# A fused SSD and cos-gated feed-forward kernel: hp in seven products in three steps of chunks 2, 3 and 4 as well

## Chip, cores, metric

One core of a Trainium2 chip. The metric is the device time of one execution in microseconds, lower is better. A time is the median of several executions; one further execution was profiled.

## The reference, cut to what matters

```python
# x (4, 8, 768, 32), a (4, 8, 768), B and C (4, 8, 768, 16); w_in (256, 2048), w_out (2048, 256); all fp32
# first block, per sequence and head, in chunks of the time axis:
log_a = np.log(np.clip(a, 1e-06, 1.0));  cum = np.cumsum(la, axis=-1)
L = np.exp(cum[:, :, :, None] - cum[:, :, None, :]) * causal
y_intra = einsum('bhij,bhjd->bhid', einsum('bhin,bhjn->bhij', Cc, Bc) * L, xc)
y_inter = einsum('bhin,bhnd->bhid', Cc, state) * np.exp(cum)[..., None]
y[:, :, sl] = y_intra + y_inter          # and state is carried to the next chunk
# second block, on y as (3072, 256):
h = y @ w_in
g = h * np.cos(h)
out = g @ w_out
```

The change touches the product y @ w_in, and the small differences that it needs.

## The kernel before

**Tiling.** The time axis of 768 is cut into six chunks of 128 (c = 0 to 5). A chunk holds 512 rows of the second block. The feed-forward runs in steps n = 0 to 95; step n belongs to chunk c = n // 16, with f = n % 16. In chunks 1 to 5 a step takes one half of the chunk's rows, u = f // 8 (256 rows), and one eighth of d_ff, j = f % 8 (256 columns of w_in). A tile hp of a step is 128 partitions by 512 columns, one PSUM bank.

**One step.** `first(n)` makes hp with four fp32 matmuls of 256 columns (L660). `wind_k` (ACT, L667) and `wind_w` (DVE, L673) reduce the argument of the cosine, `gate` (ACT, L682) takes the Sin, `gated` (DVE, L687) multiplies hp and cosine into gT. `second(n - 2)` then multiplies the gT of two steps earlier with w_out.

**Seven products.** A product of two 2x2 block matrices can be had with seven block products in place of eight, if differences and sums of the blocks are ready (Strassen's way, in Winograd's form). For o, `seven(n)` does so in every step from chunk 1 on: seven matmuls of 128 columns (L835). Its differences of gT are made in `differ(n)` on POOL (L712, L714, L715), those of w_out in `differ_w`. After the eight steps of a half chunk ACT copies the seven accumulators to ps (`take`, L847 and L848), four additions make the result (`rest`, L860: on DVE in most places, on POOL in others) and SP stores it (L863).

For hp, `first7(n)` (L759) does the same in steps 81 to 93 only, the range `sevens`. It needs differences of w_in (`differ_in`, POOL, L731, 16 instructions spread over chunks 3 and 4) and of y (`differ_y`, DVE, L741, step 79). The parts are put together by an ACT copy of the first product (L766) and four DVE additions (L772, L775, L777, L780). A step in `sevens` gates the step before it: `first_of_seven(n)` runs `wind_k(n - 1)` and the rest between and after the seven products, since hp is whole only after the additions. The step after the last of the range gates two.

**PSUM.** hp alternates between two banks (tag "h"). Within a run of seven products every third hp takes a third one, the first half of a pair of banks of the tag "scan"; the other pair of that tag holds four 128x128 accumulators of `first7` (the tile m of `pair("m")`). The two pairs of "scan" are also those of the first block's products: `inner2` (L603, f = 5), `open2` (L617, L477, f = 13) and `finish2` (L629, f = 15) compute the next chunk's y while the present chunk is in the feed-forward. o has two banks.

**Work of the first block on DVE.** Of the next chunks: `reaches` (f = 1, 2), `turn_blocks` (3, 4), `weights` (6, 7; L465), and the scans of `decays2` (8, 9, 10, 11; L375), each pair of which is followed by a load of new decay rows on SP (L165) and a product on POOL (`weigh0`, L381). `unsummed` holds the `rest` of a half chunk until its turn; in regular steps all four additions are run at once on DVE, but not in steps 10 and 11; in steps of `sevens` one addition a step on POOL.

**Order.** The program order on each engine is written out by hand in the loop over n; an engine takes its instructions in that order, and semaphores come from the data and the buffers. On SP the loads of coming chunks and the stores stand in one queue.

Of the kernel before, what the change touches and what calls it, by code (L numbers as in the profile page):

```python
# [12 lines left out]
ALU = mybir.AluOpType  # L13
# [12 lines left out]
def kernel(  # L26
# [13 lines left out]
    V, ACT, G, PE = nc.vector, nc.scalar, nc.gpsimd, nc.tensor  # L40
# [3 lines left out]
    P = 128  # L44
    NC = S // P
    DM, DF = moe_w_in.shape
    KT = DM // P
    NF = DF // P
# [28 lines left out]
    along, blocks = {}, {}  # L77
# [205 lines left out]
    for s in range(2):  # L283
# [3 lines left out]
        out=a_in, in_=a.rearrange("(u b) h (c p) -> (b h c) u p", u=NU, p=P))  # L287
# [67 lines left out]
    reach, part, yT, after = {}, {}, {}, {}  # L355
# [287 lines left out]
    NJ = NF // 2  # L643
# [78 lines left out]
    def differ_in(i, js):  # L722

        if i == len(wid):
            t = conv.tile([P, 2 * WC, 2], U32, tag="words", bufs=8, name="wid")
            wid.append(t.rearrange("p a w -> p (a w)").bitcast(FP32)
                       .rearrange("p (j f) -> p j f", j=NJ))
        g = [win4[:, k, js, e] for k in range(2) for e in range(2)]
        a_ = (g[1], g[1], g[0], g[2])[i]
        b_ = (g[3], g[0], wid[0][:, js], wid[min(i, 2)][:, js])[i]  # L730
        G.tensor_tensor(out=wid[i][:, js], in0=a_, in1=b_, op=ALU.subtract)  # L731

    def differ_y(c, i):

        if i == 0:
            yd[c] = ms[2].rearrange("p (i u m) -> p i u m", i=4, u=2)
        d = yd[c]
        y11, y12, y21, y22 = (yT[c][:, :, k, h * P:(h + 1) * P] for k in range(2) for h in range(2))
        a_ = (y12, y22, y22, y21)[i]
        b_ = (y11, y12, d[:, 0], d[:, 2])[i]  # L740
        V.tensor_tensor(out=d[:, i], in0=a_, in1=b_,  # L741
                        op=ALU.add if i in (1, 2) else ALU.subtract)

    def first7(n, to_, at6, at, between):

# [219 lines left out]
    def rest_of_loads():  # L965
# [21 lines left out]
        for k in (4, 5):  # L987
            for s in range(2):
# [4 lines left out]
    steps = {c: dict(reach=(5, 6), turn=(6, 7), inner=8, weigh=(9, 10), state=(-NF, 12),  # L993
                     decays=(8, 11, 13, 14), along=(12, 13)) if c == 2 else
             dict(reach=(1, 2), turn=(3, 4), inner=5, weigh=(6, 7), state=(0, 5),
                  decays=(8, 9, 10, 11), along=(6, 7)) for c in range(2, NC)}
    first_decays = (NF + 1, NF + 2, NF + 3, NF + 4)

    def chunks_at(n, what):
# [20 lines left out]

    sevens = range(NC * NF - 15, NC * NF - 2)
    late, at_ = [], {}
    quiet = (5, 6, 7, 8, 9, 10, 13, 14)

    def first_of_seven(n):

        i = n - sevens[0]
        if i == 0:  # L1030
            at_["hp"] = pair("hp")[:, 0]
            at_["m"] = pair("m").rearrange("p b (q m) -> p b q m", m=P)
        if n == NC * NF - NJ + LAG + 1:
            at_["hp"] = bank([P, TB], "hp", "o")
        to_ = at_["hp"] if i % 3 == 1 else bank([P, TB], "hp", "h")
        if n not in sevens:
            first(n, to_=to_)
            return
        sums, last_sum = first7(n, to_, at_["m"][:, 1, 0], at_["m"][:, 0],
                                lambda: wind_k(n - 1) if i else None)  # L1040
        if i:
            wind_w(late[0])
        sums()
        gate(late[0]) if i else None
        gated(late.pop())
        last_sum()
# [55 lines left out]
    for n in range(AHEAD, NC * NF + LAG):  # L1102
        c, f = divmod(n, NF)
        if n < NC * NF:

            if c > 0 and f in (loads_of := (6, 7, 8, 9) if c == 1 else (0, 1, 2, 3)):
                load(c + 2, loads_of.index(f))
            if n in (NF - 4, NF - 3):
                load_arow(n - NF + 8)
            if n == NF - 2:  # L1110
                for k in (4, 5):
                    for s in range(2):
                        load_x(k, s)
            if n in (NF - 1, NF):
                load_along(2, (2 * (n == NF), 2 * (n == NF) + 1))
            for e, i in chunks_at(n, "along"):
                load_along(e + 1, (2 * i, 2 * i + 1))
            if n in sevens or n - 1 in sevens:
                first_of_seven(n)
            else:  # L1120
                first(n)
            if n not in sevens and n - 1 in sevens:
                wind(n - 1)
                gate(n - 1)
                gated(late.pop())
            closing = f == NF - 1 and 1 <= c < NC - 1
            take_y = finish2(c + 1) if closing else None
            if n not in sevens:
                wind_k(n)
                wind_w(n)  # L1130
            if closing:
                take_y(0)
            for e, s in chunks_at(n - 1, "turn"):
                turn2(e, s)
            for k in units_at(n, 2):
                turn_unit(k)
            if n + 1 in piece:
                rests_of.append(grade(*piece[n + 1], later=True))
            if n not in sevens:
                gate(n)  # L1140
            while len(rests_of) > (n == AHEAD):
                rest = rests_of.pop(0)
                if rest:
                    rest()
            joins = n in piece and piece[n] in held
            if joins:
                join(*piece[n])

            behind = [lambda at=at: decays2(*at) for at in decays_at(n)]
            behind += [lambda k=2 * c - 1 + i: add_state(k) for c, i in chunks_at(n, "state")]  # L1150
            behind += [lambda c=c, b=2 * s + p: reaches(c, b) for c, s in chunks_at(n, "reach")
                       for p in range(2)]
            behind += [lambda at=at: turn_blocks(*at) for at in chunks_at(n, "turn")]
            behind += [lambda k=k, p=p: decays0(k, p) for k, at in unit_at.items()
                       for p in range(2) if at[0][p] == n]
            behind = [lambda k=2 * c + i, q=q: weights(k, q) for c, i in chunks_at(n, "weigh")
                      for q in range(2)] + behind
            behind = [lambda k=k: weights(k, 1) for k in units_at(n - 1, 3)] + behind
            if not joins and behind:
                behind.pop(0)()  # L1160
            if n + 1 in sevens or n in sevens:
                late.append(n)
            else:
                gated(n)
            if closing:
                take_y(1)
            if n == NF + 7:
                weigh0(5)
            if add_s and (n == NF - 5 or units_at(n - 1, 4)):
                exchange = add_s()  # L1170
                add_s = None
            if n == NF + 9:
                exchange()
            for do in behind:
                do()
            for i in range(4 if n == sevens[0] - 2 else 0):
                differ_y(NC - 1, i)
            if n in sevens and unsummed:
                unsummed[0](range(summed[0], summed[0] + 1), G)
                summed[0] = (summed[0] + 1) % 4  # L1180
                if summed[0] == 0:
                    unsummed.pop()
            if n not in sevens and f not in ((10, 11, 12) if c == 1 else (10, 11)):
                for do in unsummed:
                    do()
                unsummed.clear()
            for k, ((_, last_), *_) in unit_at.items():
                if last_ == n:
                    weigh0(k)
        for i, js in differ_at.get(n, ()):  # L1190
            differ_w(i, js)
        if NC - 3 <= c < NC - 1 and f in quiet:
            i, q = divmod((c - NC + 3) * len(quiet) + quiet.index(f), 4)
            differ_in(i, slice(2 * q, 2 * q + 2))
        if n == AHEAD + 1:
            second(AHEAD - LAG)
        if n >= LAG and n != AHEAD:
            second(n - LAG)
        for e, _ in chunks_at(n, "inner"):
            inner2(e)  # L1200
        for k in units_at(n, 3):
            for t in range(2):
                inner(k, t)
            if k == 3:
                at = [gs[k, s][:, 0, 2 * P:] for s in range(2)]
                sums(4, at, group)
                take_sums((4,), at)
            weights(k, 0)
        for k in units_at(n, 4):
            take_s, add_s = finish0(k)  # L1210
            take_s()
        for k in units_at(n, 1):
            reach_unit(k)
        if f == NF - 3 and 1 <= c < NC - 1:
            open2(c + 1)
        for at, e in block_loads.items():
            if at == n:
                loading = load_blocks(e)
            if at <= n < at + 12:
                next(loading)  # L1220
# [30 lines left out]
```

## Time and profile before

| | |
|---|---|
| median of 3 runs | 365.75 us (365.31 to 366.82) |
| the profiled execution, its own time | 365.62 us |
| its span | 363.8 us, 10001 instructions |
| PE (TensorE matmul) busy | 358.3 us, 98% |
| weight loads (PEld, beside PE) | 325.7 us, 90% |
| DVE busy | 262.2 us, 72% |
| POOL busy | 220.8 us, 61% |
| ACT busy | 180.9 us, 50% |
| L660 hp, four products | 664 records, 158.2 us |
| L835 o, seven products | 1106 records, 14 a step |
| L759 hp, seven products | 182 records in 13 steps |

How to read it: an fp32 matmul leaves two records, so four matmuls of `first` are eight records. Records overlap, since matmuls are pipelined, and the mean of one is longer than its share of the time; the chain of waits in order of time gives the share. The difference of 1.8 us between the execution's time and its span lies outside of the instructions. A row of the profile's groups names line, engine, operation, output <- inputs, shape and count, then busy time, mean of one, and idle time before it with what ended it. "Idle before" of an engine that nobody waits for costs nothing.

### The profile page before, as it was taken

The numbers are of one execution on the slowest core, as the hardware profiler recorded it, in microseconds if no ns is written. First come the engines' busy times: TensorE is split into PE (matmuls) and PEld (weight loads), VectorE is DVE, ScalarE is ACT, GpSimd is POOL, SyncE is SP. The second block draws the span as 40 slices with busy tenths as digits, with TensorE's granted clock in tenths as the row PEclk, the third lists the DMA queues.
The fourth block names the chain that finished last, engine by engine and source line by source line (L and its number), as shares of the span: only waits on it lengthen the run. The fifth ranks groups of instructions, "written<-read, shape, count | busy, mean of one in ns | idle before, by whom it ended". The sixth has DMA issues, their size and how long they took to land.

```text
span 363.8 us, 10001 instructions
## 1 busy us (share of the span) xinstructions
PE 358.3 (98%) x3980; PEld 325.7 (90%) x3980; DVE 262.2 (72%) x468; ACT 180.9 (50%) x337; POOL 220.8 (61%) x355
## 2 busy tenths in 40 slices
PE   8999999999999999999999999999999999999995
PEld 5788888888999999999989999999999999999995
DVE  7789988488777856977735878654877456688874
ACT  3587757444455255535335544425453534544642
POOL 5567747579767543447733458945456746475562
PEclk9999999999999999999999999999999999999999
DMA  8995957692665445315124121010010010001001
GB/s 142 254 372 132 183 128 131 105 135 61 120 100 78 92 99 84 57 46 113 21 50 70 35 56 27 0 41 10 2 31 0 2 29 4 2 1 31 1 14 46
DMA packets 97326, 26.41 MB, mean 73 GB/s; under 512 B 87328, under 2 KB 93184, under 8 KB 97280
## 3 DMA queue, kind: packets, MB, share of 16 engines
q1 hardware_dynamic: 96032, 25.38, 34.6%
q8 instruction: 31, 0.51, 0.6%
q10 hardware_dynamic: 1248, 0.39, 0.5%
q14 instruction: 15, 0.12, 0.1%
HBM read 22.36 MB, written 3.34 MB: 71 GB/s over the span
## 4 chain that ended last, share of the span: by engine, by line
PE 89%; DVE 4%; POOL 3%; ACT 2%; issue 2%; ACTq 0%; POOLq 0%; DVEq 0%
PE hp L660 36%; PE o L835 33%; PE o L795 5%; PE m L759 3%; PE hp L759 2%; PE y L629 2%; PE g L603 1%; DVE mag L261 1%; PE y L477 1%; PE y L617 1%; DVE mag L263 1%; POOL gd L714 1%; PE a_ps L364 1%; POOL gd L712 1%; PE g L456 1%
## 5 line engine op out<-in xcount | busy, mean ns | idle before, releaser
L660 PE MATMUL hp<-yT,w_in 128*128 128x256 f32 x664 | 158.2, 382 | 0.4 <-DVE gT L687 0.4
L660 PEld LDWEIGHTS hp<-yT,w_in 128*128 128x128 f32 x664 | 120.6, 190 | 16.5 <-issue 1.3
L712 POOL TENSOR_TENSOR gd<-gT 128x256 f32<-128x256 f32 x79 | 59.9, 758 | 94.7 <-DVE gT L687 84.5
L673 DVE SCALAR_TENSOR_TENSOR w<-hp,k 128x512 f32<-128x512 f32 x96 | 65.9, 687 | 58.1 <-ACT k L667 58.0
L682 ACT ACTIVATE w<-w,quarter 128x512 f32<-128x512 f32 x96 | 69.4, 723 | 69.5 <-DVE w L673 69.2
L667 ACT ACTIVATE k<-hp 128x512 int32<-128x512 f32 x96 | 57.1, 595 | 83.0 <-PE hp L660 79.8
L687 DVE TENSOR_TENSOR gT<-hp,w 128x512 f32<-128x512 f32 x96 | 65.6, 683 | 24.0 <-ACT w L682 22.1
L835 PE MATMUL o<-words,gd 128*128 128x128 f32 x474 | 66.1, 275 | 0.1
L835 PEld LDWEIGHTS o<-words,gd 128*128 128x128 f32 x474 | 59.3, 192 | 0.4 <-POOL gd L714 0.3
L835 PEld LDWEIGHTS o<-w_out,gT 128*128 128x128 f32 x316 | 46.8, 191 | 3.5
L835 PE MATMUL o<-w_out,gT 128*128 128x128 f32 x316 | 49.7, 276 | 0.0
L715 POOL TENSOR_TENSOR gd<-gT,gd 128x128 f32<-128x128 f32 x79 | 41.2, 522 | 6.2
L714 POOL TENSOR_TENSOR gd<-gT,gd 128x128 f32<-128x128 f32 x79 | 40.6, 514 | 6.2
L835 PE MATMUL o<-w_out,gd 128*128 128x128 f32 x158 | 30.6, 276 | 0.0
L835 PE MATMUL o<-words,gT 128*128 128x128 f32 x158 | 30.5, 275 | 0.0
L795 PE MATMUL o<-w_out,gT 128*128 128x256 f32 x128 | 29.9, 379 | 0.0
L375 DVE TENSOR_TENSOR_SCAN lam<-arow,unit 128x512 f32<-128x512 f32 x20 | 28.0, 1402 | 0.0
L795 PEld LDWEIGHTS o<-w_out,gT 128*128 128x128 f32 x128 | 24.2, 190 | 3.3
L835 PEld LDWEIGHTS o<-words,gT 128*128 128x128 f32 x158 | 24.0, 192 | 0.0
L835 PEld LDWEIGHTS o<-w_out,gd 128*128 128x128 f32 x158 | 24.0, 192 | 0.0
L465 DVE TENSOR_TENSOR m<-g,lam 128x512 f32<-128x512 f32 x24 | 16.2, 681 | 0.7 <-PE g L456 0.5
L271 POOL TENSOR_TENSOR w_out<-mag,last 128x512 uint32<-128x512 uint32 x8 | 10.2, 1276 | 10.1 <-DVE mag L263 10.1
(128 smaller groups left out, 373.3 us busy)
## 6 DMA issues: line engine op xcount, KB each, us to landing
words<-in_moe_w_in_dram SPq DMA_DIRECT2D x8, 512.0 KB
words<-in_moe_w_out_dram SPq DMA_DIRECT2D x8, 512.0 KB
xr<-in_x_dram SPq DMA_DIRECT2D x24, 128.0 KB
arow<-a_cut SPq DMA_DIRECT2D x10, 256.0 KB
arow<-a_cut SPq DMA_DIRECT2D x10, 252.0 KB
out_dram<-sum SPq DMA_DIRECT2D x18, 128.0 KB
bc<-in_B_dram SPq DMA_DIRECT2D x24, 64.0 KB
blocks<-in_B_dram SPq DMA_DIRECT2D x16, 32.0 KB
```

What stands on the lines that cost most here:

```text
L375: V.tensor_tensor_scan(out=lams[k][:, p, hs].rearrange(flat), data0=rows_.rearrange(flat), data1=unit0[:, hs].rearrange(flat), initial=0.0 ...
L660: PE.matmul(to_[:, e], lhsT=w_in[:, k, fs], rhs=y[:, k], start=(k == 0), stop=(k == KT - 1), skip_group_check=True)
L667: ACT.activation(k, hp[n], AF.Copy, bias=0.25, scale=INV_2PI)
L673: V.scalar_tensor_tensor(out=w, in0=hp[n], scalar=INV_2PI, in1=k, op0=ALU.mult, op1=ALU.subtract)
L682: ACT.activation(cos, cos, AF.Sin, bias=quarter, scale=TWO_PI)
L687: V.tensor_tensor(out=gT[n], in0=hp.pop(n), in1=cos, op=ALU.mult)
L712: G.tensor_tensor(out=d[:, 0:2], in0=g[:, 1:2].to_broadcast([P, 2, P]), in1=g[:, 3::-3], op=ALU.subtract)
L714: G.tensor_tensor(out=d[:, 2], in0=g[:, 0], in1=d[:, 0], op=ALU.subtract)
L715: G.tensor_tensor(out=d[:, 3], in0=g[:, 2], in1=d[:, 2], op=ALU.subtract)
L759: PE.matmul(dst[q], lhsT=w[q], rhs=y_[q], start=(q in (6, 1, 7)), stop=True, skip_group_check=True)
L795: PE.matmul(o[c, u][:, t], lhsT=g[:, 2 * e + t], rhs=w_out[:, 2 * j + e], start=(j == e == t == 0), stop=(j == NJ - 1 and e == 1), skip_gr ...
L835: PE.matmul(at[q], lhsT=a_[q], rhs=w[q], start=(j == 0 and q in starts), stop=(j == NJ - 1), skip_group_check=True)
```

## The change

Nine more steps make hp in seven products: f = 10 to 12 (u = 1, j = 2 to 4) of chunks 2, 3 and 4, that is steps 42 to 44, 58 to 60 and 74 to 76. What goes with it:

- The differences of w_in are made earlier and in three parts by columns: j = 2 to 4 in steps 27 to 30 (four instructions of 128x384), j = 0 and 1 in steps 45 to 48 (four of 128x256), j = 5 to 7 in steps 61 to 64 (four of 128x384). The 16 instructions of 128x256 in chunks 3 and 4 go.
- The differences of y for chunks 2, 3 and 4, of half u = 1 only, are made on POOL in steps f = 4 to 7, one each (128x128). For chunk 5 they stay on DVE in step 79.
- Two of the four scans `decays` of chunks 4 and 5 move from f = 10, 11 to f = 14, 15, with the load of decay rows and the `weigh0` that follow them. `along` and the rest stay.
- The sums of the half chunk that ends at f = 7 are made on POOL in steps f = 10 to 13, one addition a step, in place of all four on DVE in step f = 12; the copies to ps are issued within `first7` of step f = 10 and not at the end of step f = 9.

```diff
-    def differ_y(c, i):
+    def differ_y(c, i, eng, us=slice(0, 2)):
...
-        V.tensor_tensor(out=d[:, i], in0=a_, in1=b_,
-                        op=ALU.add if i in (1, 2) else ALU.subtract)
+        eng.tensor_tensor(out=d[:, i, us], in0=a_, in1=b_,
+                          op=ALU.add if i in (1, 2) else ALU.subtract)
...
-                  decays=(8, 9, 10, 11), along=(6, 7)) for c in range(2, NC)}
+                  decays=(8, 9, 14, 15), along=(6, 7)) for c in range(2, NC)}
...
-    sevens = range(NC * NF - 15, NC * NF - 2)
+    runs = [*(range(NF * c + 10, NF * c + 13) for c in range(2, NC - 1)),
+            range(NC * NF - 15, NC * NF - 2)]
+    sevens = {n: r for r in runs for n in r}
     late, at_ = [], {}
-    quiet = (5, 6, 7, 8, 9, 10, 13, 14)
 
     def first_of_seven(n):
 
-        i = n - sevens[0]
+        i = n - sevens.get(n, sevens.get(n - 1))[0]
...
-            for i in range(4 if n == sevens[0] - 2 else 0):
-                differ_y(NC - 1, i)
-            if n in sevens and unsummed:
+            if n == runs[-1][0] - 2:
+                for i in range(4):
+                    differ_y(NC - 1, i, V)
+            if 2 <= c < NC - 1 and 4 <= f <= 7:
+                differ_y(c, f - 4, G, slice(1, 2))
+            if unsummed and (n in sevens or summed[0]):
                 unsummed[0](range(summed[0], summed[0] + 1), G)
                 summed[0] = (summed[0] + 1) % 4
                 if summed[0] == 0:
                     unsummed.pop()
-            if n not in sevens and f not in ((10, 11, 12) if c == 1 else (10, 11)):
+            elif n not in sevens and f not in ((10, 11, 12) if c == 1 else (10, 11)):
...
-        if NC - 3 <= c < NC - 1 and f in quiet:
-            i, q = divmod((c - NC + 3) * len(quiet) + quiet.index(f), 4)
-            differ_in(i, slice(2 * q, 2 * q + 2))
+        for start, js in zip((2 * NF - 5, 3 * NF - 3, 4 * NF - 3),
+                             (slice(2, 5), slice(0, 2), slice(5, NJ))):
+            if start <= n < start + 4:
+                differ_in(n - start, js)
```

More of the change, by code (lines that the diff above doesn't have):

```diff
@@ L737, in differ_y @@
         d = yd[c]
-        y11, y12, y21, y22 = (yT[c][:, :, k, h * P:(h + 1) * P] for k in range(2) for h in range(2))
+        y11, y12, y21, y22 = (yT[c][:, us, k, h * P:(h + 1) * P] for k in range(2)
+                              for h in range(2))
         a_ = (y12, y22, y22, y21)[i]
-        b_ = (y11, y12, d[:, 0], d[:, 2])[i]
-        V.tensor_tensor(out=d[:, i], in0=a_, in1=b_,
-                        op=ALU.add if i in (1, 2) else ALU.subtract)
+        b_ = (y11, y12, d[:, 0, us], d[:, 2, us])[i]
+        eng.tensor_tensor(out=d[:, i, us], in0=a_, in1=b_,
+                          op=ALU.add if i in (1, 2) else ALU.subtract)
     def first7(n, to_, at6, at, between):
```

## The prediction

> **What bounds the kernel now.** I read the page first (busy shares, then the chain of waits), then the busy time by stretch, then the chain in order of time for the stage that is edited, then single engines there.
>
> ```profile
> span 363.8 us, 10001 instructions
> ...
> PE 358.3 (98%) x3980; PEld 325.7 (90%) x3980; DVE 262.2 (72%) x468; ACT 180.9 (50%) x337; POOL 220.8 (61%) x355
> ...
> PE 89%; DVE 4%; POOL 3%; ACT 2%; issue 2%; ACTq 0%; POOLq 0%; DVEq 0%
> ```
>
> TensorE is busy for 98% of the span and holds 89% of the chain that ended last; no other engine passes 72%. The stretches cut at the first matmul of each chunk say it more sharply (columns: length, then busy time of PE, weight load, DVE, ACT, POOL, granted clock, DMA share, GB/s):
>
> ```profile
> 134.35:191.76 57.41, 57.41 (x674) 53.17 (x673) 39.48 (x71) 26.30 (x49) 30.76 (x51) 1.00 0.36 66
> 191.76:249.19 57.43, 57.43 (x673) 53.16 (x673) 39.30 (x71) 26.50 (x50) 36.24 (x57) 1.00 0.19 36
> 249.19:305.81 56.62, 56.62 (x609) 52.47 (x609) 34.91 (x67) 26.38 (x49) 32.41 (x56) 1.00 0.05 11
> 308.82:349.70 40.88, 40.88 (x366) 40.80 (x365) 31.68 (x76) 21.42 (x42) 23.94 (x43) 1.00 0.03 8
> ```
>
> The first three are chunks 2, 3 and 4; the last is the stretch of steps 81 to 93. PE is busy for the whole of each (57.41 of 57.41) at clock 1.00. So in these stages time is the sum of TensorE's instructions, and work taken off DVE or POOL gives nothing. The chain in order of time shows what a step costs:
>
> ```profile
> 175.16 1.73 PE hp L660 x8
> 176.89 1.56 PE o L835 x14
> 178.45 1.73 PE hp L660 x8
> ...
> 312.53 0.89 PE m L759 x8
> 313.87 1.72 PE o L835 x14
> 315.81 0.89 PE m L759 x8
> 317.15 1.56 PE o L835 x14
> 318.93 0.89 PE m L759 x8
> ```
>
> A regular step (44 here: 175.16 to 178.45) takes 3.29 us: eight records of L660 (four fp32 matmuls of 256 columns, two records each) in 1.73, fourteen records of L835 in 1.56. A step with hp in seven products (L759) takes 318.93 - 315.81 = 3.12. Seven products of 128 columns cost the same whether they make o or hp: 1.56.
>
> **The change part by part.** Step n is 16c + f.
>
> *hp in seven products in nine more steps* (42 to 44, 58 to 60, 74 to 76). By weight loads the last eleven steps of the present run take (349.70 - 315.31)/11 = 3.126 us, so a step saves 3.29 - 3.126 = 0.164; nine save 1.48 us. Here a rule speaks against the change. The row: 14 records of 128 columns in 1.56 us (111.5 ns each), 8 of 256 columns in 1.73 (216 ns each). The Trainium skill, "TensorE: Matmul & The Clock Gate", section "Back-to-back issue gap", says that a stream of weight load and matmul pairs is slower at 128 columns than the isolated gap of about 56 ns: 81 ns each, and 131 at 512. Taking a record as two such matmuls (111.5 is about 2 x 56), the rule would make 14 x 162 = 2.27 us of the seven, and, with some 98 ns at 256 between its two figures, 8 x 196 = 1.57 of the four: an estimate of 0.70 us lost per step, 6.3 in nine. The trace has the very instruction mix at 3.126 us per step, so the row decides.
>
> *Entering a run.* The present run's first two steps took 3.21 and 3.28 instead of 3.126, 0.24 together. In the first, product 3 waited for ACT's copy L766, late behind the Sin of the step before; in the second, o waited for the copies of the last sums to ps, which stood behind L667. In the new runs the copies stand in the first step, straight after L766. By rows: step 42 begins at 168.3, ACT's Sin ends at 169.19, L766 (0.26) at about 169.4, the lower copy (0.46) at about 169.8, and seven(40) wants its bank at 168.3 + 1.56 = 169.86. Nothing waits, or 0.1 does. Bounds: 0 and 0.24 per run; I take 0.05, since row 42 is nearer than 81. Three runs: -0.15.
>
> *Leaving a run.* The step after it (45, 61, 77) gates two steps. The present exit, step 94, shows how late:
>
> ```profile
> 349.70 1.60 PEld L660 LDWEIGHTS hp<-yT,w_in 128*128 128x128 f32 x8
> 353.01 0.69 DVE L687 TENSOR_TENSOR gT<-hp,w 128x512 f32<-128x512 f32 x1 [0.86 <-ACT w L682]
> ```
>
> gated(93) ends at 353.70, 4.00 us after the step's start S. In the new runs the bank of that hp is taken again by the step after next (46, 62, 78), which would begin at S + 3.29. But the step in between ends with open2: the chain has 1.63 us there in chunks 2 and 3 (181.74 to 183.37) and 0.84 in chunk 4 (296.58 to 297.42), so it begins at S + 4.92 and S + 4.13. Margin 0.9 and 0.1 us: cost 0, with an upper bound of 0.7 (4.00 - 3.29) if that cover were gone. open2 itself needs the two pairs that the run used: the last reading of m ends at S + 0.13, before its turn at S + 3.29.
>
> *DVE.* Each seven-step adds L772, L775, L777 and L780, 0.29 + 0.42 + 0.43 + 0.29 = 1.43 us, to 0.69 + 0.69. The present run fits 2.8 into 3.126. Out of its way go the scans (1.22 to 1.37 us) of steps 42, 43, 58 and 59, and the sums of steps 44, 60 and 76 (0.42 + 1.89 us, to POOL). The scans land in steps 46, 47, 62, 63: 0.69 + 1.22 + 0.69 = 2.6 of 3.29, as steps 40 to 43 do it now without a PE stall. ACT gets nine copies of 0.26; no more.
>
> *POOL.* Per run it gets four 128x128 differences of y at f = 4 to 7 (0.46 each; 1.85 with the differences of gT makes 2.3 of 3.29), then 0.73 x 3 + 0.46 of sums, spread over four steps as steps 82 to 85 do now. Differences of w_in: 16 of 256 columns (0.73) leave chunks 3 and 4; eight of 384 come, priced at 1.0 (128 columns 0.46, 256 0.73, the same slope on; bounds 0.73 and 1.46), and four of 256. A POOL instruction is held up while DVE scans:
>
> ```profile
> 168.35 1.22 DVE L375 TENSOR_TENSOR_SCAN lam<-arow,unit 128x512 f32<-128x512 f32 x1
> 168.51 1.31 POOL L715 TENSOR_TENSOR gd<-gT,gd 128x128 f32<-128x128 f32 x1
> 171.19 0.46 POOL L714 TENSOR_TENSOR gd<-gT,gd 128x128 f32<-128x128 f32 x1
> ```
>
> 0.46 became 1.31. The two heavy places by hand: in steps 27 to 30 POOL idles 1.2 to 2.4 us before each next difference (122.47 and 126.07 wait for DVE), so a piece of 1.0 fits, with 0.25 over where a scan lies on it, against 2.3 us between the difference of step 27 being ready (120.7) and its use (123.05). At the end of chunk 3, from S of step 61, gd(n) being the differences of gT of step n: gd(60) to 6.0, gd(61) to 8.1, sum 8.6, w_in 9.6 and a scan 10.6, gd(62) 12.4 (13.3 with the next scan), w_in 14.3, gd(63) 16.1; seven(63) wants it at 12.91 + 3.29 + 1.73 + 0.45 = 18.4. 2.3 us to spare: 0. It is covered by PE's own queue; were the cover gone, each 1.0 us piece would show, 8 us in all.
>
> *SP.* The store of a half chunk's sums is issued after POOL's fourth sum, S + 8.6 (186.5) instead of 182.15; behind it stand block loads (2.0 + 2.7 us of issue) and the moved arow load (about 1.3), done by about 194. The blocks are turned in step 52, after 201; arow is scanned in step 62. Cost 0.
>
> Sum: -1.48 + 0.15 = -1.33. The profiled execution took 365.62 (span 363.8), 0.13 under the median 365.75: 365.62 - 1.33 = 364.29; against the median 364.4. About 0.5%, 1.8 us, is what a measurement of this kernel can tell from no change, so -0.37% lies within it.
>
> **Rivals.**
> - *Entry waits as in the present run* (same direction, smaller): 0.24 in each of three runs, -1.48 + 0.72 = -0.76, 365.0. For it: the only entry on record. Against: its second wait came from a copy queued behind L667, which is not so in step 42. Chance 0.13.
> - *The exit becomes the bound* (slower). Place: first(46), first(62), first(78), waiting for the bank of a hp that is gated late; then the next step behind scan and gate. Decides when gated(44) slips past S + 4.92, and past S + 4.13 in chunk 4, where only 0.1 us is left. Price: if the gating slips by one scan and one gT (1.22 + 0.69 = 1.9), PE stalls 1.9 - 0.9 = 1.0 in chunks 2 and 3 and 1.8 in chunk 4, 3.8 in all; less 1.33 that is 365.75 + 2.5 = 368.2. For it: the present exit is followed by a single regular step, not by scans. Against: the rows above. Chance 0.10.
> - *The run does not run at its own pace*: the y differences come too late and product 4 of step 42 waits for them. POOL's differences of gT of step 39 end at 165.36 now, one piece of 0.46 later is 165.9; step 42 begins at 168.3. With a wait of 0.44 per run the gain would be cancelled: 365.7. Chance 0.05.
> - *More than the sum* (over 1.83 us): PE has no idle time in chunks 2 to 4 to give back, so only scatter between runs (365.31 to 366.82) can show it. Chance 0.08.
>
> **How the numbers follow.** The main case, -1.1 to -1.5 us, has 0.64, and with scatter runs from 364.0 to 364.8; it is in "same". The smaller gain and the cancelled gain (0.18) are there too: same 0.81. Faster 0.08, slower 0.11 (the exit, and a wait I have not seen). The range goes up to 365.7 to hold the second and third case, and down to 363.9.
>
> **What would show it.** L759 with 308 records instead of 182, L660 with 592 instead of 664; seven-steps of 3.12 to 3.2 us in the chain at 168, 226 and 284; PE busy for the whole of each chunk, chunks 2, 3 and 4 each shorter by 0.4 to 0.5. Wrong would be: "PE hp L660 <- DVE gT L687" or "PE o L835 <- POOL gd" among the waits with more than 0.3 us; a first seven-step over 3.4; a gap before first(46), (62) or (78).

## The result, and the profile after

| | median | against the kernel before |
|---|---|---|
| changed kernel, first comparison | 364.43 us (15 runs) | 365.75 (15 runs); ratio 0.9951, 95% interval 0.9935 to 0.9966 |
| changed kernel again (e1) | 364.39 us (11 runs) | 365.49 (28 runs); ratio 0.9972, 0.9963 to 0.9981 |
| predicted | 364.4 us | ratio 0.9964 |

The medians lie 1.32 and 1.10 us apart, the forecast was 1.33. The intervals mean a gain of 1.2 to 2.4 us in the first comparison and of 0.7 to 1.4 in the second; the forecast ratio lies in both. The change makes the kernel faster by about a third of a per cent, less than the 0.5% that the forecast set as a clear difference.

The first profiled execution of the changed kernel was disturbed in chunk 1 by a late load, before any edited step (369.8 us of span), and is left out of the ratio, which is not the quotient of the medians. So the lines below are of the same kernel in e1, whose profiled execution took 364.50 us (before: 365.62); in the disturbed one chunks 2, 3 and 4 take the same as there, 56.92, 56.99 and 56.13 us. In the changed file the lines from 736 on stand one lower: L759 is now L760, L835 L836, L860 L861, L766 L767. The page first:

```profile
span 362.7 us, 10169 instructions
...
PE 356.1 (98%) x4034; PEld 325.6 (90%) x4034; DVE 271.0 (75%) x492; ACT 182.5 (50%) x346; POOL 235.0 (65%) x375
...
PE 92%; POOL 3%; DVE 1%; DMA 1%; issue 1%; ACT 0%; SPq 0%; POOLq 0%; DVEq 0%; ACTq 0%
...
L660 PE MATMUL hp<-yT,w_in 128*128 128x256 f32 x592 | 141.3, 382 | 0.2 <-issue 0.2
```

Then the groups of L760 with shapes kept apart (busy time, mean ns of one):

```profile
L760 PE MATMUL m<-m,wid 128*128 128x128 f32 x132 | 18.3, 275 | 0.0
L760 PE MATMUL hp<-yT,w_in 128*128 128x128 f32 x88 | 17.0, 275 | 0.0
L760 PE MATMUL hp<-yT,wid 128*128 128x128 f32 x44 | 8.6, 277 | 0.0
L760 PE MATMUL m<-m,w_in 128*128 128x128 f32 x44 | 8.5, 275 | 0.0
```

132 + 88 + 44 + 44 = 308 records of L760, and 592 of L660: nine more steps in seven products, as forecast. The stretches of chunks 2, 3, 4, and of chunk 5 to the last matmuls (length, busy PE, weight load, DVE, ACT, POOL, clock, DMA):

```profile
134.63:191.55 56.92, 56.92 (x692) 53.29 (x691) 41.08 (x79) 26.89 (x53) 36.48 (x60) 1.00 0.29 53
191.55:248.55 57.00, 57.00 (x692) 53.37 (x691) 41.65 (x79) 26.91 (x53) 38.54 (x64) 1.00 0.26 48
248.55:304.68 56.13, 56.13 (x628) 52.60 (x627) 37.30 (x75) 26.91 (x52) 33.52 (x59) 1.00 0.05 12
304.68:357.23 52.55, 52.55 (x446) 51.81 (x445) 39.67 (x89) 26.44 (x51) 31.45 (x56) 1.00 0.05 12
```

Against 57.41, 57.43 and 56.62 the three chunks are 0.49, 0.43 and 0.49 us shorter, 1.41 together, and PE is busy for the whole of each. DVE has 1.6 to 2.4 us more to do in each, POOL up to 5.7 in chunk 2 (36.48 against 30.76), and of all this PE shows 0.09 us in chunk 3. The rest of the span agrees: chunk 2 begins 0.28 later (134.63 against 134.35; the starts of the other kernels below scatter from 133.7 to 135.3, apart from e7's), and from the first step of chunk 5 to the last matmuls it is 52.55 against 52.53.

The chain in order of time through the first new run:

```profile
165.58 1.73 PE hp L660 x8
167.31 1.56 PE o L836 x14
168.87 0.22 PE hp L760 x2
169.09 0.89 PE m L760 x8
169.99 0.45 PE hp L760 x4
170.43 1.56 PE o L836 x14
172.00 0.22 PE hp L760 x2
...
175.12 0.22 PE hp L760 x2
...
178.25 1.73 PE hp L660 x8
179.98 1.56 PE o L836 x14
181.54 0.84 PE y L617 x53
182.38 0.79 PE y L477 x53
183.17 1.92 PE hp L660 x8
```

The run begins at 168.87 and ends at 178.25: 9.38 us for three steps, 3.13 each, where three regular steps take 9.87. There is no wait at its entry (in the present run of chunk 5 the first two steps still take 3.21 and 3.28), and none at its exit: first(46) follows open2 (L617, L477) at once.

### The profile page after: what moved, and what is told of

Its sections match the earlier page's. It is cut to its first block, busy times and chain, and to the rows that moved or that the text cites. A ratio compares the mean times of both kernels' runs of the same rounds, so it can differ in the third digit from the quotient of the medians.

```text
span 369.8 us, 10169 instructions
## 1 busy us (share of the span) xinstructions
PE 359.4 (97%) x4034; PEld 327.8 (89%) x4034; DVE 270.8 (73%) x492; ACT 182.3 (49%) x346; POOL 233.0 (63%) x375
## 4 chain that ended last, share of the span: by engine, by line
PE 83%; DVE 4%; POOL 3%; ACT 2%; DMA 2%; SPq 2%; issue 2%; DVEq 0%; ACTq 0%; POOLq 0%
PE o L836 31%; PE hp L660 30%; PE m L760 5%; PE o L796 5%; PE hp L760 4%; PE y L629 2%; PE g L603 1%; DMA blocks<-in_C_dram 1%; SPq L150 1%; POOL gd L712 1%; DVE mag L261 1%; DMA bc<-in_B_dram 1%; POOL gd L714 1%; DVE w L673 1%; PE y L617 1%
## 5 line engine op out<-in xcount | busy, mean ns | idle before, releaser
L660 PE MATMUL hp<-yT,w_in 128*128 128x256 f32 x592 | 143.0, 386 | 0.4 <-DVE gT L687 0.4
L660 PEld LDWEIGHTS hp<-yT,w_in 128*128 128x128 f32 x592 | 108.8, 192 | 15.6 <-issue 1.6
L712 POOL TENSOR_TENSOR gd<-gT 128x256 f32<-128x256 f32 x79 | 59.8, 758 | 89.4 <-DVE gT L687 74.3
L836 PE MATMUL o<-words,gd 128*128 128x128 f32 x474 | 66.1, 276 | 0.1
L836 PEld LDWEIGHTS o<-words,gd 128*128 128x128 f32 x474 | 59.4, 192 | 0.3 <-POOL gd L714 0.3
L836 PE MATMUL o<-w_out,gT 128*128 128x128 f32 x316 | 50.1, 278 | 0.0
L836 PEld LDWEIGHTS o<-w_out,gT 128*128 128x128 f32 x316 | 46.6, 193 | 3.2
L714 POOL TENSOR_TENSOR gd<-gT,gd 128x128 f32<-128x128 f32 x79 | 40.4, 512 | 6.2
L715 POOL TENSOR_TENSOR gd<-gT,gd 128x128 f32<-128x128 f32 x79 | 39.0, 494 | 6.2
L836 PE MATMUL o<-w_out,gd 128*128 128x128 f32 x158 | 30.7, 276 | 0.0
L836 PE MATMUL o<-words,gT 128*128 128x128 f32 x158 | 30.6, 275 | 0.0
L375 DVE TENSOR_TENSOR_SCAN lam<-arow,unit 128x512 f32<-128x512 f32 x20 | 29.8, 1489 | 0.0
L836 PEld LDWEIGHTS o<-words,gT 128*128 128x128 f32 x158 | 24.0, 192 | 0.0
L836 PEld LDWEIGHTS o<-w_out,gd 128*128 128x128 f32 x158 | 24.0, 192 | 0.0
L760 PE MATMUL m<-m,wid 128*128 128x128 f32 x132 | 18.3, 275 | 0.0
L760 PE MATMUL hp<-yT,w_in 128*128 128x128 f32 x88 | 17.0, 275 | 0.0
```

Of the source, the lines that this page charges most:

```text
L375: V.tensor_tensor_scan(out=lams[k][:, p, hs].rearrange(flat), data0=rows_.rearrange(flat), data1=unit0[:, hs].rearrange(flat), initial=0.0 ...
L660: PE.matmul(to_[:, e], lhsT=w_in[:, k, fs], rhs=y[:, k], start=(k == 0), stop=(k == KT - 1), skip_group_check=True)
L712: G.tensor_tensor(out=d[:, 0:2], in0=g[:, 1:2].to_broadcast([P, 2, P]), in1=g[:, 3::-3], op=ALU.subtract)
L714: G.tensor_tensor(out=d[:, 2], in0=g[:, 0], in1=d[:, 0], op=ALU.subtract)
L715: G.tensor_tensor(out=d[:, 3], in0=g[:, 2], in1=d[:, 2], op=ALU.subtract)
L760: PE.matmul(dst[q], lhsT=w[q], rhs=y_[q], start=(q in (6, 1, 7)), stop=True, skip_group_check=True)
```

## The experiments

Two theories stood against each other at first. Theory 1: the gain is TensorE's sum, and it is kept because scans, copies and open2 lie where they cover the rest. Theory 2: work taken off DVE, or put elsewhere on POOL, gives something besides. Ratios are to the kernel before in the same comparison; "stage" is the length of chunks 2, 3 and 4 in the chain.

| | ratio (95% interval) | chunks 2, 3, 4 (us) |
|---|---|---|
| before | 1 | 57.41, 57.43, 56.62 |
| e1 changed kernel | 0.9972 (0.9963 to 0.9981) | 56.92, 57.00, 56.13 |
| e2 moves only | 1.0021 (1.0011 to 1.0031) | 57.64, 57.43, 56.62 |
| e3 scans stay | 1.0015 (1.0003 to 1.0026) | 57.80, 57.79, 56.13 |
| e4 copies early | 1.0034 (1.0022 to 1.0047) | 57.76, 57.83, 56.96 |
| e5 exit bare | 1.0047 (1.0032 to 1.0062) | 57.87, 58.21, 56.92 |
| e6 runs of four | 1.0344 (1.0320 to 1.0368) | 62.70, 62.67, 59.05 |
| e7 w_in twice | 1.0000 (0.9981 to 1.0020) | 56.92, 113.95 for both others |
| e8 runs of four, other bank | 1.0046 (1.0028 to 1.0063) | 57.82, 58.27, 57.23 |
| e9 scans moved only | 1.0002 (0.9988 to 1.0015) | 57.51, 57.41, 56.62 |
| e10 w_in moved only | 0.9988 (0.9973 to 1.0003) | 57.42, 57.41, 56.63 |

**e1: the changed kernel again.** No edit.

> The changed kernel once more, for a second profile and a narrower time. Theory 1 (the gain is TensorE's sum: nine steps at 0.164 us less, no entry or exit wait): 1.3 to 1.5 us under the kernel before, ratio 0.9960 to 0.9965, and chunks 2, 3 and 4 each 0.44 to 0.49 us shorter in the chain. Theory 2 (the work taken off DVE, or moved on POOL, gives something besides): 1.8 us or more, ratio 0.995, with a gain outside of the nine steps.

Measured: 0.43 to 0.49 us less in each of the three stages, 1.41 together, as in Theory 1; by the medians 1.10 and by the ratio 1.0, which is under its 1.3 to 1.5. The start of chunk 2, 0.28 us later in this execution, scatters by more than these figures differ. Theory 2's 1.8 is outside of this interval. The first comparison's interval doesn't rule it out, but the stages do: nothing is gained outside of the nine steps.

**e2: the moves without the seven products.**

```diff
-    runs = [*(range(NF * c + 10, NF * c + 13) for c in range(2, NC - 1)),
-            range(NC * NF - 15, NC * NF - 2)]
+    runs = [range(NC * NF - 15, NC * NF - 2)]
```

> The moves of the change without its point: the scans at f = 14 and 15, the differences of w_in in steps 27 to 30, 45 to 48 and 61 to 64, the differences of y on POOL (made, and not used), but hp in four products in all steps of chunks 2 to 4, and with it the sums on DVE in step f = 12 as before. Theory 1: the time of the kernel before, within 0.3 us, since PE has no idle time there to give back. Theory 2: a part of the gain shows already here, 0.4 us or more under the kernel before.

Measured: 0.8 us slower than before (366.34 against 365.49). Theory 2 falls: the moves bring nothing by themselves. Theory 1's "within 0.3" missed too. In the profile chunk 2 is 0.23 longer, in step 47 (5.12 against 4.90), where L629 takes 1.64 and not 1.41 with no wait recorded; steps 81 to 85 of the last run are 0.37 longer; and the last eight records (L888) take 1.97 and not 1.74. One thing seen on the way is who starts first on a scan. Here is POOL and DVE in step 46 of e2, then of e1:

```profile
186.29 0.73 POOL L731 TENSOR_TENSOR wid<-w_in 128x256 f32<-128x256 f32 x1
186.39 1.70 DVE L375 TENSOR_TENSOR_SCAN lam<-arow,unit 128x512 f32<-128x512 f32 x1
```

```profile
186.43 1.21 DVE L375 TENSOR_TENSOR_SCAN lam<-arow,unit 128x512 f32<-128x512 f32 x1
186.44 1.73 POOL L731 TENSOR_TENSOR wid<-w_in 128x256 f32<-128x256 f32 x1
```

In e2 POOL's piece of w_in started 0.1 us ahead and the scan took 1.70; in e1 the scan started 0.01 ahead and the piece took 1.73 in place of 0.73. The later of the two pays, by a little less than the overlap (the scan 0.49 for 0.63, the piece 1.00 for 1.20). What of this reaches PE in e2 the chain doesn't show, which was the reason for e9 and e10.

**e3: scans at f = 10 and 11 as before.**

```diff
-                  decays=(8, 9, 14, 15), along=(6, 7)) for c in range(2, NC)}
+                  decays=(8, 9, 10, 11), along=(6, 7)) for c in range(2, NC)}
```

> The changed kernel with the scans back at f = 8, 9, 10 and 11, so that chunks 2 and 3 have a scan in each of the first two seven-steps. Theory 1: DVE then has 0.69 + 1.43 + 0.69 + 1.22 = 4.0 us to do in a step of 3.126, and hp's additions come late: 0.5 to 1.1 us lost in each of two chunks, 1 to 2.2 us over the changed kernel, most or all of the gain gone. Rival: the lag is taken up by the later steps, in which DVE has room, and the time is that of the changed kernel within 0.2 us; then the move of the scans was not needed.

Measured: chunks 2 and 3 lose 0.88 and 0.79 against e1, chunk 4 (which has no scan) nothing; 1.67 together, and the ratios differ by 0.0043, 1.6 us. The size is as Theory 1 had it, the way is another. The chain in step 43, and from the rows of DVE the scan that lies on it:

```profile
171.18 0.60 DVE gT L687
...
171.91 1.72 POOL gd L712
...
173.70 0.47 POOL gd L714
...
174.21 1.38 PE o L836 x10
```

```profile
171.88 1.22 DVE L375 TENSOR_TENSOR_SCAN lam<-arow,unit 128x512 f32<-128x512 f32 x1
```

The scan follows gated(41) on DVE and so starts just as POOL starts on its differences of that gT. L712 takes 1.72 in place of 0.73, and o (L836) waits for POOL's L714. It is not hp's additions that are late: the gT that follows them starts 2.43 us after the run's first product, and 2.42 in e1.

**e4: the copies to ps ahead of the run.**

```diff
-        if n + LAG + 1 in sevens:
+        if n + LAG + 1 in runs[-1]:
             finished.append(take)
```

> The changed kernel with the two copies to ps at the end of step f = 9, ahead of the first seven-step on ACT, in chunks 2 to 4 (the last run keeps its place). Theory 1 on entering a run: the copies (1.05 us) stand between the Sin of the step before and the copy of the first product, product 3 waits for that about 0.8 us, in each of three runs: 2.4 us over the changed kernel, slower than the kernel before by about 1. Rival: PE has other products to go on with and the place of the copies is worth under 0.3 us in all.

Measured: 0.84, 0.83 and 0.83 over e1 in the three stages, 2.50; by the ratios 2.3. ACT and weight loads in step 42:

```profile
168.84 0.72 ACT L682 ACTIVATE w<-w,quarter 128x512 f32<-128x512 f32 x1 [0.76 <-DVE w L673]
169.47 0.46 ACT L848 COPY ps<-o 128x384 f32<-128x384 f32 x1
169.82 0.59 ACT L849 COPY ps<-o 128x512 f32<-128x512 f32 x1
170.30 0.28 ACT L767 COPY m<-hp 128x128 f32<-128x128 f32 x1
170.63 0.30 PEld L760 LDWEIGHTS hp<-yT,wid 128*128 128x128 f32 x2 [0.76 <-ACT m L767]
```

Sin, two copies, then the copy of the first product, and the weight load of product 3 waits 0.76 for that. In e1 the same copy ends at 169.64 and that weight load begins at 169.71, so the entry is free by 0.07 us; the place of two copies decides over more than the whole gain.

**e5: the exit without open2 behind it.**

```diff
-        if f == NF - 3 and 1 <= c < NC - 1:
+        if f == (NF - 3 if c == 1 else NF - 2) and 1 <= c < NC - 1:
             open2(c + 1)
```

> The changed kernel with open2 of chunks 3 to 5 one step later (f = 14 and not 13), so that the step that leaves a run is not followed by open2. Theory 1 on leaving a run: first(46) then wants the bank of hp(44) at S + 3.29 and gets it at S + 4.0 (in the changed kernel's trace gated(44) ends 3.99 us after S): 0.7 us of waiting for gT in each of three runs, 2.1 us over the changed kernel and about 0.9 over the kernel before. Rival: the banks are not what the exit hangs on, and the time is that of the changed kernel within 0.3 us.

Measured: 0.95, 1.21 and 0.79 over e1 in the stages, 2.95; by the ratios 2.7. The chain at the first exit:

```profile
180.84 0.70 DVE gT L687
...
181.68 1.97 PE hp L660 x8
183.65 1.56 PE o L836 x14
```

hp waits for gT, as expected: 0.59, 0.84 and 0.56 us at the three exits, 1.99 together, where 2.1 was forecast. The eight records after each wait take 1.97 where they take 1.73 in the stream, 0.24 more, and L629 of the next step 1.54 and 1.55 and not 1.41 in chunks 2 and 3. Those two were not in the forecast, so the kernel lands 1.9 us over the kernel before by the medians and not 0.9.

**e6: runs of four.**

```diff
-    runs = [*(range(NF * c + 10, NF * c + 13) for c in range(2, NC - 1)),
+    runs = [*(range(NF * c + 10, NF * c + 14) for c in range(2, NC - 1)),
...
-                             (slice(2, 5), slice(0, 2), slice(5, NJ))):
+                             (slice(2, 6), slice(0, 2), slice(6, NJ))):
```

and open2 at f = 14 as in e5.

> Runs of four steps (f = 10 to 13) in chunks 2 to 4, open2 after the step that leaves them (f = 14), and the differences of w_in split as j = 2 to 5 (steps 27 to 30), 0 and 1, 6 and 7. Theory 1: three more steps at 0.164 and open2 again behind the exit: 0.49 us under the changed kernel, about 1.6 to 1.9 under the kernel before. Rival: the step that leaves the run now has a scan on DVE besides the two gatings (0.69 x 4 + 0.29 + 1.22 = 4.3 us) and the later differences on POOL come too late: no gain over the changed kernel, or 0.5 us lost.

Measured: 12.8 us over the kernel before. A miss, and by neither theory's cause; the waits name it:

```profile
PE y L617 <- DVE gT L687: 8.5, 3, 2.9
```

open2 waits up to 2.9 us for gT, once in each of three runs: 8.5 us of the 14.4 that the three stages lose against e1. About half of the rest is in the eight records of the next hp (L660). Here are their stretches after the three waits (columns as above; the clock is the third figure from the end):

```profile
189.50:192.67 3.17, 3.17 (x17) 2.36 (x23) 0.00 (x0) 0.00 (x0) 0.71 (x2) 0.61 0.99 177
252.87:256.58 3.71, 3.71 (x17) 2.52 (x22) 0.00 (x0) 0.00 (x0) 0.16 (x1) 0.50 0.00 0
313.83:315.75 1.92, 1.92 (x16) 1.44 (x22) 0.00 (x0) 0.00 (x0) 0.88 (x2) 1.00 0.00 0
```

After the waits of chunks 2 and 3 (2.85 and 2.88 us) the granted clock read 0.61 and 0.50, and the records took 3.17 and 3.71 us; after that of chunk 4 (2.73 us) it read 1.00 and they took 1.92, as behind open2 without a wait. Chunk 2 has a further 1.14 us within L629 for which the profile names no releaser. So a long wait can cost more than itself; what decides whether the clock falls, no run here tells.

The wait itself comes from a bank. Every third hp of a run takes a bank of the pair that open2 needs. With three steps the hp of the leaving step is the fourth and takes the ordinary bank; with four steps it is the fifth and takes the pair's, and that hp is gated last of all.

**e8: runs of four, the leaving step in its own bank.**

```diff
-        to_ = at_["hp"] if i % 3 == 1 else bank([P, TB], "hp", "h")
+        to_ = at_["hp"] if i % 3 == 1 and (n in sevens or n > 90) else bank([P, TB], "hp", "h")
```

> Runs of four steps as in e6, but hp of the step that leaves the run (46, 62, 78) in a bank of its own tag and not in the pair that open2 takes next. Theory (e6's 14 us came from open2 waiting for gT of the step that leaves the run, through that bank): y L617 no longer waits for gT; first(46) takes the bank of hp(44), gated in step 45 about 0.8 us after first(46) could begin, so 3 x 0.8 - 0.49 = 1.9 us over the changed kernel, about 0.7 over the kernel before. Rival: what cost e6 its time was the load of the step that leaves the run (two gatings and a scan), and 5 us or more stay over the kernel before.

Measured: the wait of L617 is gone, with 11 of e6's 12.8 us, but 1.7 over the kernel before are left, and not the 0.7 of the forecast. Step 45 shows what comes in place of that wait:

```profile
181.89 0.70 DVE gT L687
...
182.73 1.97 PE hp L660 x8
184.69 1.56 PE o L836 x14
```

first(46) starts at 182.73, 3.82 us after first7(45) and not 3.12: it waited for gT of step 44. The wait is 0.7 (0.8 expected; 0.7 and 1.0 in chunks 3 and 4), again with the slower records behind it. Against e1 the stages lose 0.90, 1.27 and 1.10, 3.27 together, where 1.9 was forecast; the slower records behind the waits (0.24 each) and longer L629 in chunks 2 and 3 are what it left out. So a run of four, in this arrangement of the banks, costs more than the 0.164 us that its fourth step saves; a run of three leaves by a bank that is free in time.

**e7: each difference of w_in twice.**

```diff
             if start <= n < start + 4:
                 differ_in(n - start, js)
+                differ_in(n - start, js)
```

> The changed kernel with each of the twelve differences of w_in made twice (the second time over the first, same values): 8 x 1.0 + 4 x 0.73 = 10.9 us more for POOL in steps 27 to 30, 45 to 48 and 61 to 64. Theory 1 (POOL's part lies beside PE with 2.3 us to spare at the end of chunk 3): nothing in steps 27 to 30 and 45 to 48, and at steps 63 to 65 four pieces of 1.0 less 2.3 at most: 0 to 1 us over the changed kernel in all. Rival (POOL is near the bound there): each place shows 1 us or more, 3 us and up in all.

Measured, in an execution that lost 3.3 us ahead of chunk 2: chunk 2 takes 56.92, as in e1; chunks 3 and 4 take 113.95 against 113.13, 0.82 more. The chain shows where, in chunk 3's last steps and after:

```profile
257.52 1.00 POOL wid L731
258.52 0.70 POOL gd L712
...
261.31 1.00 POOL wid L731
262.32 0.70 POOL gd L712
```

The chain runs through POOL alone from 244.85 to 263.0, then through DVE, and PE waits once in chunks 3 and 4: 0.58 us for gT before hp of step 69, with the eight records after it again at 1.97, which makes up the 0.82. The kernel as a whole is 1.0 over e1 by the ratios, within Theory 1's 0 to 1. So with 4 us more POOL becomes the bound there and PE loses under 1 us; with the pieces once it has the room that the prediction gave it. A piece of 384 columns takes 1.00, and 1.92 where a scan lies on it.

**e9 and e10: which of the moves costs e2 its time.** e9 is the kernel before with `decays=(8, 9, 14, 15)`; e10 is the kernel before with the three places of `differ_in` from the change in place of the sixteen instructions.

> The kernel before with only the two scans of chunks 4 and 5 moved from f = 10, 11 to f = 14, 15. Together with e10 this parts the 0.6 to 0.8 us that the moves alone cost in e2. Theory a (the scans are the cost: in step 47 and its neighbours they fall on a place with less cover): 0.3 us or more over the kernel before. Theory b (the pieces of w_in are the cost: they start ahead of a scan and hold it up): the time of the kernel before within 0.2.

> The kernel before with only the differences of w_in in steps 27 to 30, 45 to 48 and 61 to 64 in place of sixteen in chunks 3 and 4. Theory a: the time of the kernel before within 0.2. Theory b: 0.3 us or more over it. Theory c (neither; e2's loss comes from both on the same steps, or from where instructions fall, which shifts with every edit): both e9 and e10 within 0.2.

Measured: 1.0002 and 0.9988, both intervals with 1 in them. That is nearest to Theory c: no cost is shown for either move, though e10 lies 0.3 to 0.4 us under the kernel before and not within 0.2, and e9's interval (up to 0.5 us over it) leaves room for a small one. In chunk 2 of e9 L629 of step 47 takes 1.52, a part of what it takes in e2.

e9's last run has 0.29 in steps 84 and 85, as e2 has 0.30, though no line of that stage differs from the kernel before. The rows show where: o of step 84 takes 1.81 (1.82 in e2) and not 1.56, behind a gT that starts late. Here is that gT on DVE with the addition ahead of it, before and in e9:

```profile
318.13 0.43 DVE L777 TENSOR_TENSOR hp<-m 128x256 f32<-128x256 f32 x1
318.56 0.69 DVE L687 TENSOR_TENSOR gT<-hp,w 128x512 f32<-128x512 f32 x1
```

```profile
317.57 0.43 DVE L777 TENSOR_TENSOR hp<-m 128x256 f32<-128x256 f32 x1
318.35 0.69 DVE L687 TENSOR_TENSOR gT<-hp,w 128x512 f32<-128x512 f32 x1 [0.34 <-POOL sum L860]
```

In both the Sin that gT needs ended 0.11 us before the addition did. The profile puts the 0.34 down to POOL's sum, which gT doesn't read. So this part of e2's loss is not a wait that the change makes; why gT starts late in one execution and not in the other stays open.

## Why the prediction was right

- *Nine steps at 0.164 us.* 3.13 per step measured in each new run, 1.41 us in the three chunks against 1.48. Chunk 3 gives 0.43 and not 0.49 because o of step 61 takes 1.65 in place of 1.56, ahead of which gT of step 59 had started 0.34 late, beside POOL's sum: the same event as in step 84 of e9. The rule of the Trainium skill ("TensorE: Matmul & The Clock Gate", section "Back-to-back issue gap"), from which the prediction estimated a loss of 6.3 us by taking a record as two of the page's matmuls, is not what fp32 products do in this stream: 14 records in 1.56 us, in the new runs as in the old.
- *Entering a run.* 0 measured, 0.05 taken. The rows of ACT were read rightly, to 0.1 us, and 0.07 us is what was left over: e4 shows the cost when the copies stand elsewhere, 0.83 a run against 0.8 forecast.
- *Leaving a run.* 0 measured. gated(44) ended 3.99 us after S, against 4.00 from step 94 (gated(60) 4.34, after the late gT, still within its cover), and e5 shows that open2 is the cover: without it 2.95 us.
- *DVE.* The scans had to move: e3. Here the step was right in its size and wrong in its reason. I counted DVE's own time in a step (4.0 of 3.126); what reached PE was POOL held up by the scan. The sums put on POOL fit between the differences.
- *POOL.* 384 columns were priced at 1.0 and took 1.00. The room at the end of chunk 3 was there: four more microseconds cost 0.8 (e7), at step 69 and not at seven(63), for which the 2.3 were reckoned.
- *SP.* POOL's fourth sum ended at 186.49, as forecast (186.5), and nothing in chunks 2 to 4 waited for a load.
- *The rivals.* The slower one, the exit, was a true danger with a true price, and the kernel stays clear of it by open2. The rival of a larger gain is not borne out by e1. In the rival of late y differences one time was read too low: the last difference met a scan, took 1.37 and not 0.46 us and ended at 166.98, still 1.6 us before the run's first weight load.
- *Luck.* That the first medians lie within 0.01 us of the forecast is luck, since the second pair gives 1.10. The sum rests on the stages: 1.48 less 0.15 for entries, where 1.41 and no entry wait were measured.
- *What the sum doesn't explain:* e2 is slower than e1 by 1.8 us by the ratios, 1.95 by the medians, where the nine steps account for 1.41. The traces place the rest: 0.23 in L629 of step 47, 0.34 in the last run (0.30 of it behind the late gT), 0.23 in the last eight records; against these, chunk 2 begins 0.53 earlier in e2. What makes these places slower stays open.

## What to carry to other kernels

Where one engine is busy without a gap, count the change in that engine's own records, from a place in the same trace that already does it; the rest of the work is then only to name, for each move, what keeps it hidden. Those covers are narrow and belong to places: two copies put ahead of a third, two scans left four steps earlier in each of two chunks, or one more step in a run each cost more here (2.5, 1.7 and 3.3 us in the stages) than the nine cheaper steps bring (1.4). Ask of every buffer that a run borrows who takes it next, and what the last step of the run leaves in it.

## What the hardware showed besides

- Where a scan on DVE and an elementwise instruction on POOL lie on each other, the later one takes longer, whichever it is, by the overlap less 0.1 to 0.2 us. POOL's 128x128 goes from 0.46 to 1.31 us (overlap 1.06), 128x384 from 1.00 to 1.92 (1.13); a scan from 1.21 to 1.70 where POOL was first by 0.1 us (0.63).
- After a wait of 0.6 to 1.0 us, the next eight records of four 256-column products take 1.97 us in place of 1.73, at a granted clock of 1.00, so such a stall costs about 0.24 us more than itself (e5, e7, e8). They take 1.92 after the first block's small products without a wait. Why was not taken apart.
- After waits of 2.85 and 2.88 us the granted clock fell to 0.61 and 0.50 for the next eight records (3.17 and 3.71 us); after one of 2.73 us it stayed at 1.00 (e6).
- The 128 small matmuls of L629 take 1.41 us in most places and 1.52 to 1.64 in some (e2, e5, e8, e9), with no wait recorded.
